# Phase one in chunks of 512 and 192 tokens, 112 rows of v, and a new order of the work

## The chip, the cores and the metric

The kernel runs on one core of a Trainium2 chip. Its time is device microseconds of one execution. TensorE (PE, its weight loads PEld), VectorE (DVE), ScalarE (ACT), GpSimd (POOL) and SyncE (SP) each work through a list of their own in order; DMA queues move the data.

## The reference, cut to what matters

```python
# attention: B, H, S, D = 4, 8, 576, 64; factor 4
out_d = sm_attn(mean4(q), mean4(k), mean4(v))      # 144 x 144 scores per head
out_local = sm_attn(q, k, v, |i - j| < 4)          # a band
x = repeat(out_d, 4) + out_local                   # then (B, S, 512)
# channel mix (phase one, and the gate of phase two)
xk = mu_k * x + (1 - mu_k) * x_prev
xr = mu_r * x + (1 - mu_r) * x_prev
v = relu(xk @ w_k) ** 2 @ w_v                      # 512 -> 1024 -> 512
x1 = sigmoid(xr @ w_r) * v
# conv GLU (phase two)
h = relu(x1 @ w_in)                                # 512 -> 1024
out = (h * sigmoid(conv3(h, conv_w))) @ w_out      # 1024 -> 512
```

All of it is float32 in and out, over 4 x 576 = 2304 tokens.

## The kernel before

**Stages.** The kernel first does the attention of batch 0 (heads in two groups, `gp`), in two pieces of 192 and 384 tokens. Phase one (`first_mix`, `mix`) multiplies by `w_k`, squares, multiplies by `w_v` and writes v to DRAM, in chunks of tokens: `chunks_` holds 192, 384 and then four of 432. The attention of batches 1 to 3 (`attend_batch`) runs between the matmuls of chunks 1 to 3. Phase two (`load_chunk`, `gate`, `hidden`, `outp`) reads x and v back and runs in five chunks of 384 or 512 tokens. In the first chunk the weights are used as float32 as they arrive (L919, L949). From the second on every product is made of three single-pass matmuls on a high and a low part of each operand (`for g, (wt, xs) in enumerate(((0, 0), (1, 0), (0, 1)))`), so a chunk of phase one has 96 matmuls in `up` (L983, 8 tiles of 12) and 96 in `down` (L1033, 4 tiles of 24, in halves), whatever its length; each has a weight load of 128x128 of its own. In phase two the lines are L1324 (gate), L1372 (hidden) and L1467 (out).

**Parts.** A weight block of 128x512 is read (L409), put together from two words by ScalarE and DVE (L396, L415, L399), copied to its high part on either engine (L435 or L437) and subtracted on DVE for the low part (L441). `mix_prep` forms xk of a chunk (L880 ScalarE, L888 DVE) and its two parts (L897, L902) in `late["xk"]`, one buffer. After `up` come relu (L1002), square, copy (L1014 or L1016) and subtraction (L1022) into the ring `k2` of nine buffers.

**Attention.** DVE sums keys and queries by four (L526). Scores (L564 band, L629 down-sampled) go through maxima, exponent and sums; transposes (L703, L759) land in PSUM and are copied by ScalarE (L709, L764). v comes as `vw`, 128 rows: two blocks of 64 positions, of which a block's window uses 38. For batch 0 a fold of `vw` by matmul (L499) replaces the sums by four; L786 and L805 are the products with v, L727 the down-sampled one, and its copy is L739.

**Order.** Each piece of work is a `step` with an engine, a cost and the keys that it reads and writes; the list `ORDER` gives the one order in which all steps are emitted, so that each engine's list follows from it. A step that may run on two engines runs on the second if its number stands in the set `SECOND`. DMAs are issued by the engine named in the step, nearly all by SP. Ten pieces of filler matmuls (L1089) stand in PE's list before the first scores.

**Memory.** `tmp` holds 8 tiles of NT tokens (a chunk's working tiles); `sq` the squares of chunk 0; `wr` the parts of `w_r`; at the end of the attention its pool is given up for phase two's weights, hidden tiles and a tile `v`.

Of the kernel before, what the change touches and what calls it, by code (L numbers as in the profile page):

```python
# [20 lines left out]
NFILL = 10  # L21


ORDER = [
# [178 lines left out]
def act(n):  # L203
    return 0.155 + 0.93e-3 * n
# [6 lines left out]
def pe(n):  # L211
    return 14.5e-3 + 0.4167e-3 * n
# [6 lines left out]
def tile_local_attention__then__channel_mix__then__conv_glu(  # L219
# [29 lines left out]
    NB = len(starts)  # L249
    PB = BQ // FAC  # L250
    NH = S // 3
    NT = 3 * S // 4
    ROW = -(-NT // 64) * 64
    chunks_ = [(0, NH), (NH, S - NH)] + [(t, NT) for t in range(S, B * S, NT)]
    K2 = 9
# [1314 lines left out]
```

## Time and profile before

| | us |
|---|---|
| median of three timed runs | 557.69 (556.16 to 558.6) |
| profiled execution, whole time | 556.9 |
| its span, first to last instruction | 554.8 |
| PE busy in the span | 538.7 |
| DVE busy | 366.3 |
| ACT busy | 300.3 |

The span is what the trace shows; 2.1 us of the profiled execution's time lie around it. Busy time is the time in which at least one instruction of the engine is under way. A matmul's record covers its whole passage through the array, so records overlap; the price of one in a dense stream is the distance between starts, which the chain of waits gives as a piece's length over its count.

### The profile page before, as it was taken

What the parts mean: (1) busy time and instruction counts of PE and PEld (TensorE: products, weight loads), DVE (VectorE), ACT (ScalarE), POOL (GpSimd) and SP (SyncE); (2) the same over time, 40 slices, a digit from 0 to 9 for tenths busy, and PEclk for the clock granted to TensorE, in tenths of its full rate; (3) what the DMA queues carried; (4) which work ended last, traced back from release to release, by engine and by line L of the source; (5) the groups of instructions that cost most, each with busy time, mean ns of one, the idle gap of its engine ahead of it and who ended that gap; (6) DMA issues with size and microseconds to landing.
All of it is one profiled execution on the core that took longest, in us unless ns stands there. A gap on an engine that the chain in (4) does not pass through costs nothing.

```text
span 554.8 us, 12885 instructions
## 1 busy us (share of the span) xinstructions
PE 538.7 (97%) x5364; PEld 479.4 (86%) x5364; DVE 366.3 (66%) x689; ACT 300.3 (54%) x676; POOL 43.5 (8%) x181
## 2 busy tenths in 40 slices
PE   6899899999999999999999999999999999999996
PEld 3788789899898999999999998888888888899985
DVE  4699897675675385456366698579747867766750
ACT  2888676356556555464566646455535443442441
POOL 5001010110101000000000001002001101100000
PEclk9999999999999999999999999999999999999999
DMA  8577883477364614413616022232022000010021
GB/s 325 209 249 205 331 252 104 125 236 223 91 207 126 193 60 142 143 57 129 223 38 222 34 76 77 76 115 95 1 64 107 19 1 2 0 58 21 0 77 57
DMA packets 25402, 66.14 MB, mean 119 GB/s; under 512 B 2688, under 2 KB 8320, under 8 KB 24320
## 3 DMA queue, kind: packets, MB, share of 16 engines
q1 hardware_dynamic: 23616, 62.37, 32.5%
q0 software_dynamic: 1728, 2.95, 3.2%
q8 instruction: 42, 0.69, 0.5%
q14 instruction: 16, 0.13, 0.1%
HBM read 51.15 MB, written 14.16 MB: 118 GB/s over the span
## 4 chain that ended last, share of the span: by engine, by line
PE 91%; DMA 3%; DVE 3%; ACT 1%; issue 1%; SPq 0%; ACTq 0%; DVEq 0%
PE a L1467 18%; PE mm L983 17%; PE mm L1033 17%; PE mm L1372 9%; PE a L1372 9%; PE mm L1324 4%; PE a L1324 4%; PE a L805 3%; PE mm L919 2%; DMA st_d<-in_moe_w_v 2%; DMA vw<-in_vw 2%; PE a L703 1%; PE a L727 1%; PE a L564 1%; PE a L759 1%; PE a L629 1%
## 5 line engine op out<-in xcount | busy, mean ns | idle before, releaser
L983 PE MATMUL mm<-xk,wk 128*128 128x432 f32 (+1 forms) x480 | 97.0, 357 | 0.8 <-issue 0.8
L1033 PE MATMUL mm<-k,wv 128*128 128x432 f32 (+1 forms) x480 | 95.6, 356 | 0.0
L1033 PEld LDWEIGHTS mm<-k,wv 128*128 128x128 f32 x480 | 88.3, 188 | 3.9 <-issue 0.7
L983 PEld LDWEIGHTS mm<-xk,wk 128*128 128x128 f32 x480 | 88.0, 188 | 4.1 <-issue 1.1
L1467 PE MATMUL a<-wk,wv 128*128 128x512 f32 x342 | 81.0, 389 | 0.0
L1467 PEld LDWEIGHTS a<-wk,wv 128*128 128x128 f32 x342 | 64.2, 188 | 13.3
L1372 PE MATMUL mm<-k,wi 128*128 128x512 f32 (+2 forms) x240 | 52.0, 368 | 0.0
L1372 PE MATMUL a<-k,wi 128*128 128x512 f32 (+2 forms) x240 | 51.9, 368 | 0.0
L1372 PEld LDWEIGHTS mm<-k,wi 128*128 128x128 f32 x240 | 44.0, 188 | 5.8
L1372 PEld LDWEIGHTS a<-k,wi 128*128 128x128 f32 x240 | 43.9, 188 | 5.6
L1439 ACT ACTIVATE tmp<-tmp 128x513 f32<-128x513 f32 (+1 forms) x40 | 23.6, 592 | 36.3 <-DVE tmp L1433 36.1
L1002 ACT ACTIVATE tmp<-mm 128x432 f32<-128x432 f32 (+1 forms) x40 | 20.8, 522 | 26.1 <-PE mm L983 11.8
L399 DVE SCALAR_TENSOR_TENSOR st_f<-st_f,st_d 128x512 uint32<-128x512 uint32 x28 | 19.3, 689 | 23.1 <-ACT st_d L415 23.1
L1442 DVE SCALAR_TENSOR_TENSOR tmp<-tmp,h 128x384 f32<-128x384 f32 (+3 forms) x64 | 26.9, 456 | 7.2 <-ACT tmp L1439 5.8
L1022 DVE TENSOR_TENSOR k<-tmp,k 128x432 fp32r<-128x432 f32 (+1 forms) x40 | 23.5, 595 | 9.9 <-ACT k L1014 8.8
L1433 DVE SCALAR_TENSOR_TENSOR tmp<-h,cw_sb,tmp 128x513 f32<-128x513 f32 (+1 forms) x40 | 28.0, 700 | 1.8
L1430 DVE SCALAR_TENSOR_TENSOR tmp<-h,cw_sb,tmp 128x513 f32<-128x513 f32 (+1 forms) x40 | 28.0, 700 | 1.8
L1453 DVE TENSOR_TENSOR wv<-tmp,wv 128x512 fp32r<-128x512 f32 (+1 forms) x32 | 20.0, 628 | 11.6 <-ACT wv L1451 11.4
L391 POOL DMA_DIRECT2D vd<-in_vp x18 | 14.7, 817 | 162.1 <-DMA vd<-in_vp 96.9
L1429 DVE TENSOR_SCALAR tmp<-h,cw_sb 128x513 f32<-128x513 f32 (+1 forms) x40 | 18.4, 460 | 12.2 <-ACT h L1409 11.3
L1482 ACT ACTIVATE st_d<-a 128x512 f32<-128x512 f32 x18 | 10.5, 595 | 27.4 <-PE a L1467 23.7
L1451 ACT CAST wv<-tmp 128x512 fp32r<-128x512 f32 (+1 forms) x32 | 17.9, 571 | 11.8 <-DVE tmp L1442 11.6
(174 smaller groups left out, 874.8 us busy)
## 6 DMA issues: line engine op xcount, KB each, us to landing
vw<-in_vw SPq DMA_DIRECT2D x7, 1152.0 KB, 6.5
kq<-in_kq SPq DMA_DIRECT2D x6, 1152.0 KB, 6.4
x_d<-xT SPq DMA_DIRECT2D x16, 288.0 KB, 3.4
out_dram<-st_d SPq DMA_DIRECT2D x18, 256.0 KB, 2.1
st_d<-in_moe_w_k SPq DMA_DIRECT2D x8, 512.0 KB, 4.3
st_d<-in_moe_w_v SPq DMA_DIRECT2D x8, 512.0 KB, 4.8
st_d<-in_moe_w_in SPq DMA_DIRECT2D x8, 512.0 KB, 3.8
st_d<-in_moe_w_out SPq DMA_DIRECT2D x8, 512.0 KB, 4.5
```

What stands on the lines that cost most here:

```text
L983: nc.tensor.matmul(pst[:, 0:n], lhsT=wk_t[wt][:, kt, mt * P:(mt + 1) * P], rhs=late["xk"][:, xs, kt, 0:n], start=(kt == 0 and g == 0), sto ...
L1002: lambda r=r, pst=pst: nc.scalar.activation(r, pst[:, 0:n], AF.Relu), (), [pk, rk],
L1022: lambda e, r=r, j=j: e.tensor_sub(late["k2"][1][:, j, 0:n], r, late["k2"][0][:, j, 0:n].bitcast(F32)),
L1033: nc.tensor.matmul(pst[:, 0:n], lhsT=wv_t[wt][:, kt, mt * P:(mt + 1) * P], rhs=late["k2"][xs][:, at[kt], 0:n], start=(kt == 0 and g == 0), ...
L1324: nc.tensor.matmul(pst[:, 0:n], lhsT=late["wr"][wt][:, kt, mt * P:(mt + 1) * P], rhs=r_t(c, xs, kt)[:, 0:n], start=(kt == 0 and g == 0), s ...
L1372: nc.tensor.matmul(pst[:, 0:n], lhsT=late["wi"][wt][:, kt, mt * P:(mt + 1) * P], rhs=x1s(xs, kt)[:, 0:n], start=(kt == 0 and g == 0), stop ...
L1430: nc.vector.scalar_tensor_tensor(out=cv, in0=tap(0), scalar=cw[:, 0, mt:mt + 1], in1=cv, op0=ALU.mult, op1=ALU.add)
L1433: nc.vector.scalar_tensor_tensor(out=cv, in0=tap(2), scalar=cw[:, 2, mt:mt + 1], in1=cv, op0=ALU.mult, op1=ALU.add)
L1439: step("ACT", act(m), lambda: nc.scalar.activation(cv, cv, AF.Tanh, scale=0.5), (), [cvk])
L1442: nc.vector.scalar_tensor_tensor(out=gf[:, o:q], in0=cv[:, o + j:q + j], scalar=1.0, in1=tap(1)[:, o + j:q + j], op0=ALU.add, op1=ALU.mult,)
L1453: ("DVE",), (dve(m),), lambda e: e.tensor_sub(gh_t(1, j)[:, 0:m], gf, gh_t(0, j)[:, 0:m].bitcast(F32)),
L1467: nc.tensor.matmul(pst, lhsT=xs[:, tt * P:(tt + 1) * P], rhs=wo[wt][:, kt, :], start=(kt == 0 and g == 0), stop=(kt == KF - 1 and g == 2),)
```

## The change

The chunks of phase one are 192, 384, 512, 512, 512 and 192 tokens (before: 192, 384 and four of 432). `k2` has eight buffers instead of nine, each now for 512 tokens. To make room, `w_r`'s parts move to a pool that opens when `sq` is given up, phase two's tile `v` and one of the two tanh buffers go to `tmp` and to the late pool. `vw` has 112 rows in DRAM and SBUF, and the fold uses those. `mus`, the mixing factors, are loaded over ScalarE's queue. For batch 0 the copies out of PSUM of the scores, the probabilities and the down-sampled output, and the scaling of chunk 0's x, may run on ScalarE or DVE. The planner's cost of a matmul is changed, and `ORDER` and `SECOND` are new lists.

In the first twelve DMAs of SP's list the order was: kq (both of group 0), kq (second half of group 0), kq (both of group 1), vw 0, vw 1, w_k 0, mus, kq (second half of group 1), w_k 2, w_k 1. It is now: kq (four pieces), vw 0, w_k 1, w_k 0, vw 1, w_k 2, and then the two second halves of kq; mus come over ScalarE. On DVE's list two sums of the second half's kq, the bits of w_k 3, the subtraction of w_k 2 and one block of maxima now stand before the last step of chunk 0's mix.

```diff
+VR = 112
 def pe(n):
-    return 14.5e-3 + 0.4167e-3 * n
+    return (13.4e-3 if n == 512 else 14.0e-3 if n in (382, 384) else 15.7e-3 if n > 300 else 11.6e-3) + 0.4167e-3 * n
...
-    NT = 3 * S // 4
+    NT = 4 * P
     ROW = -(-NT // 64) * 64
-    chunks_ = [(0, NH), (NH, S - NH)] + [(t, NT) for t in range(S, B * S, NT)]
-    K2 = 9
+    chunks_ = [(0, NH), (NH, S - NH)]
+    while chunks_[-1][0] + chunks_[-1][1] < B * S:
+        t = sum(chunks_[-1])
+        chunks_.append((t, min(NT, B * S - t)))
+    K2 = 8
...
+        def copy(eng, o, i):
+            if eng is nc.vector:
+                eng.tensor_copy(o, i)
+            else:
+                nc.scalar.copy(o, i)
+
+        def any_step(n, f, r, w, slack):
+            if b == 0:
+                step(("ACT", "DVE"), (act(n), 0.12 + 1.0e-3 * n), f, r, w, slack=slack)
+            else:
+                step("ACT", act(n), lambda: f(nc.scalar), r, w, slack=slack)
...
-            load(t.rearrange("p e h d -> p (e h d)"), vw[b, gp], NB // 2 * 4 * D, (), [k], SL[0])
+            load(t[0:VR].rearrange("p e h d -> p (e h d)"), vw[b, gp], NB // 2 * 4 * D * VR // P, (), [k], SL[0])
...
-                                pv[q:q + m, c], lhsT=z[:, 64 - o + q:64 - o + q + m],
-                                rhs=g["vw"][0][:, e].rearrange("p h d -> p (h d)"),
+                                pv[q:q + m, c], lhsT=z[0:VR, 64 - o + q:64 - o + q + m],
+                                rhs=g["vw"][0][0:VR, e].rearrange("p h d -> p (h d)"),
...
-                step("ACT", act((e - a) * P), cp, (), pks + [(ptk, a)], slack=SL[i0 > 0])
+                any_step((e - a) * P, cp, (), pks + [(ptk, a)], SL[i0 > 0])
...
-    step("SP", 0.2, lambda: nc.sync.dma_start(out=mus[:, 0:2], in_=mu), (), ["mus0"])
+    step("ACT", 0.45, lambda: nc.scalar.dma_start(out=mus[:, 0:2], in_=mu), (), ["mus0"])
...
-        late["wr"] = several(mid, 2, [P, KM, DM], F32R, "wr")
...
+    def open_wr():
+        sq_pool.release()
+        late["wrp"] = wrp = tc.alloc_tile_pool(name="wrp", bufs=1, reuse_waits="tile")
+        late["wr"] = several(wrp, 2, [P, KM, DM], F32R, "wr")
...
     def v_t(i, kt):
-        return cutout(st_d[1 + kt // 2], kt % 2 * CH, CH, F32) if i else late["v"][0][:, kt]
+        return cutout(st_d[1 + kt // 2], kt % 2 * CH, CH, F32) if i else tmp[:, kt]
...
+    def cv_t(i):
+        return cutout(tmp, KM * NT + 2 * CH, CH + 1, F32) if i else late["cv"][0]
```

## Rows read from the trace of the kernel before

**Rows 1.** The page's head: span, and busy time of the engines (share, instructions).

```profile
span 554.8 us, 12885 instructions
PE 538.7 (97%) x5364; PEld 479.4 (86%) x5364; DVE 366.3 (66%) x689; ACT 300.3 (54%) x676; POOL 43.5 (8%) x181
```

**Rows 2.** Stretches: from:to us, length, engines' busy us, granted clock, DMA share, GB/s.

```profile
4.00:12.00 8.00, 6.71 (x90) 3.40 (x93) 4.78 (x11) 1.20 (x5) 5.25 (x25) 1.00 1.00 382
12.00:24.00 12.00, 11.66 (x313) 9.07 (x315) 6.76 (x20) 7.91 (x23) 0.00 (x0) 1.00 0.65 252
...
28.25:55.00 26.75, 25.55 (x603) 23.06 (x601) 25.14 (x57) 22.66 (x60) 2.56 (x3) 0.96 0.73 226
55.00:77.00 22.00, 19.01 (x463) 17.02 (x458) 19.66 (x35) 16.28 (x41) 1.60 (x2) 1.00 0.83 294
...
27.00:30.40 3.40, 3.40 (x57) 2.96 (x50) 3.37 (x8) 1.49 (x5) 0.00 (x0) 0.53 0.83 272
```

**Rows 3.** Waits of PE: waiting line, what ended it, us in total, times, longest.

```profile
PE mm L499 <- DMA vw<-in_vw: 1.3, 1, 1.3
PE a L703 <- DVE pd L673: 1.3, 1, 1.3
```

**Rows 4.** The chain that ended last: start us, length us, what.

```profile
95.99 2.23 PE a L805 x144
...
210.12 18.80 PE mm L1033 x96
...
389.41 21.76 PE a L1467 x96
```

**Rows 5.** PE near 77 us (timeline), and L983's groups: busy, mean ns.

```profile
76.95 0.30 PEld L983 LDWEIGHTS mm<-xk,wk 128*128 128x128 f32 x2
76.95 0.44 PE L983 MATMUL mm<-xk,wk 128*128 128x384 f32 x1
...
L983 PEld LDWEIGHTS mm<-xk,wk 128*128 128x128 f32 x480 | 88.0, 188 | 4.1 <-issue 1.1
L983 PE MATMUL mm<-xk,wk 128*128 128x384 f32 x96 | 18.3, 340 | 0.8 <-issue 0.8
```

**Rows 6.** Groups of DVE and ACT by line and shape: busy us, mean ns.

```profile
L824 DVE COPY xT<-a 128x192 f32<-128x192 f32 x2 | 0.7, 359 | 1.3 <-PE a L805 1.3
L441 DVE TENSOR_TENSOR wk<-st_f,wk 128x512 fp32r<-128x512 f32 x12 | 8.3, 688 | 1.0 <-ACT wk L435 0.9
L437 DVE CAST wk<-st_f 128x512 fp32r<-128x512 f32 x5 | 2.1, 423 | 0.1
L526 DVE TENSOR_REDUCE kqd_f<-kq_f 128x96 f32<-128x384 f32 x2 | 1.1, 548 | 0.0
L888 DVE SCALAR_TENSOR_TENSOR tmp<-xT,mus,tmp 128x192 f32<-128x192 f32 x4 | 1.6, 413 | 0.0
L673 DVE TENSOR_TENSOR pd<-pd,sums 128x720 f32<-128x720 f32 x4 | 3.6, 904 | 0.1
L709 ACT COPY pdt<-a 80x768 f32<-80x768 f32 x2 | 1.6, 788 | 1.3 <-PE a L703 1.3
L709 ACT COPY pdt<-a 80x512 f32<-80x512 f32 x2 | 1.2, 581 | 1.7 <-PE a L703 1.7
L764 ACT COPY pt<-a 128x512 f32<-128x512 f32 x14 | 8.3, 590 | 5.2 <-PE a L759 5.2
L764 ACT COPY pt<-a 128x256 f32<-128x256 f32 x2 | 0.8, 375 | 0.0
```

**Rows 7.** DMA issues up to 18 us: KB each, median us to landing.

```profile
vw<-in_vw SPq DMA_DIRECT2D x1, 1152.0 KB, 8.7
mus<-in_mu SPq DMA_DIRECT2D x1, 4.0 KB, 11.3
```

**Rows 8.** PE's timeline around the first matmul on weights: start us, us.

```profile
23.70 0.90 PE L805 MATMUL a<-pt,vw_f 38*64 38x32 f32 x48
...
28.25 0.69 PE L919 MATMUL mm<-tmp,st_f 128*128 128x192 f32 x1
```

More of the change, by code (lines that the diff above doesn't have):

```diff
@@ L380, in tile_local_attention__then__channel_mix__then__conv_glu, with load @@
     step("POOL", 4.7, make_picks, (), ["picks"])
-    def load(o, i, words, r, w, slack=1.0, rows=P):
-        step("SP", dma_us(words, rows), lambda: nc.sync.dma_start(out=o, in_=i), r, w, slack=slack)
+    def load(o, i, words, r, w, slack=1.0, rows=P, k=1.0):
+        step("SP", k * dma_us(words, rows), lambda: nc.sync.dma_start(out=o, in_=i), r, w, slack=slack)
     def load_sum(o, planes, words, keys, slack, rows=P):
@@ L471, in loads @@
                     len(prs) * (e - a), (),
-                    [(k, i, pr) for pr in prs for i in ({0, half} if whole else {i0})], SL[i0 > 0],
+                    [(k, i, pr) for pr in prs for i in ({0, half} if whole else {i0})], SL[i0 > 0], P, 1.0,
                 )
@@ L706, in down_out, with cp @@
                 step("PE", 0.218 * (e - a) + TAIL, f, [(pdk, 0), (pdk, 1)], pks, slack=SL[i0 > 0])
-                def cp(a=a, e=e, pv=pv):
-                    nc.scalar.copy(
-                        pdt[:, :, a:e].rearrange("p k c s -> p k (c s)"), pv[:HC, :, 0:(e - a) * P]
-                    )
-                step("ACT", act(2 * (e - a) * P), cp, (), pks + [(pdtk, a)], slack=SL[i0 > 0])
+                def cp(eng, a=a, e=e, pv=pv):
+                    copy(eng, pdt[:, :, a:e].rearrange("p k c s -> p k (c s)"), pv[:HC, :, 0:(e - a) * P])
+                any_step(2 * (e - a) * P, cp, (), pks + [(pdtk, a)], SL[i0 > 0])
             if b == 0 and i0 == 0:
@@ L736, in down_out, with cp @@
             whole = m // BQ * BQ
-            def cp():
-                nc.scalar.copy(od[:, :, 0:whole], po[:, :, 0:whole])
+            def cp(eng):
+                copy(eng, od[:, :, 0:whole], po[:, :, 0:whole])
                 if m > whole:
-                    nc.scalar.copy(od[:, :, whole:m], po[:, :, nq * BQ - (m - whole):nq * BQ])
-            step("ACT", act(2 * whole), cp, (), pks + [odk], slack=SL[i0 > 0])
+                    copy(eng, od[:, :, whole:m], po[:, :, nq * BQ - (m - whole):nq * BQ])
+            any_step(2 * whole, cp, (), pks + [odk], SL[i0 > 0])
         def local_out(i0, i1):
@@ L761, in local_out, with cp @@
                 step("PE", 0.109 * (e - a) + TAIL, f, g["sk", i0], pks, slack=SL[i0 > 0])
-                def cp(a=a, e=e, pst=pst):
-                    nc.scalar.copy(pt[:, a:e].rearrange("p i r -> p (i r)"), pst[:, 0:(e - a) * P])
-                step("ACT", act((e - a) * P), cp, (), pks + [(ptk, a)], slack=SL[i0 > 0])
+                def cp(eng, a=a, e=e, pst=pst):
+                    copy(eng, pt[:, a:e].rearrange("p i r -> p (i r)"), pst[:, 0:(e - a) * P])
+                any_step((e - a) * P, cp, (), pks + [(ptk, a)], SL[i0 > 0])
             over = b == 0 and i0 == 0
@@ L875, in mix_prep, with scaled @@
             xs = [("xT", b % 2, kt, c) for b, a, e in parts for c in (0, half) if (c == 0 or e > NH)]
-            def scaled(t=t, kt=kt):
+            def scaled(eng, t=t, kt=kt):
                 for b, a, e in parts:
                     o = b * S + a - t0
-                    nc.scalar.activation(
-                        t[:, o:o + e - a], xT[b % 2][:, kt, a:e], AF.Copy, scale=mus[:, 2, kt:kt + 1])
-            step("ACT", act(n) + 0.1 + 0.3 * (len(parts) - 1), scaled, xs + ["mus"], [tk])
+                    to, by, m = t[:, o:o + e - a], xT[b % 2][:, kt, a:e], mus[:, 2, kt:kt + 1]
+                    if eng is nc.vector:
+                        eng.tensor_scalar_mul(to, by, m)
+                    else:
+                        nc.scalar.activation(to, by, AF.Copy, scale=m)
+            if i == 0:
+                step(("ACT", "DVE"), (act(n) + 0.1, dve(n)), scaled, xs + ["mus"], [tk])
+            else:
+                step(
+                    "ACT", act(n) + 0.1 + 0.3 * (len(parts) - 1),
+                    lambda scaled=scaled: scaled(nc.scalar), xs + ["mus"], [tk],
+                )
             def whole(t=t, f=f, kt=kt):
@@ L1115, in tile_local_attention__then__channel_mix__then__conv_glu @@
     late["two"] = True
-    by_columns(w_r, lambda: late["wr"][0], lambda: late["wr"][1], KM, range(KM), "wr", ["mid"])
+    def open_wr():
+        sq_pool.release()
+        late["wrp"] = wrp = tc.alloc_tile_pool(name="wrp", bufs=1, reuse_waits="tile")
+        late["wr"] = several(wrp, 2, [P, KM, DM], F32R, "wr")
+    step("", 0.0, open_wr, ["mid"], [k for k in prog.writer if root(k) == "sq"] + ["wrp"])
+    by_columns(w_r, lambda: late["wr"][0], lambda: late["wr"][1], KM, range(KM), "wr", ["wrp"])
     store_x(0)
@@ L1139, in tile_local_attention__then__channel_mix__then__conv_glu @@
     att_keys = [k for k in prog.writer if root(k) in names]
-    sq_keys = [k for k in prog.writer if root(k) == "sq"]
     def open_late():
-        sq_pool.release()
         att.release()
-        late["low"] = low = tc.alloc_tile_pool(name="low", bufs=1, reuse_waits="tile")
-        late["v"] = several(low, 1, [P, KM, CH], F32, "v")
         wb = late["pool"] = tc.alloc_tile_pool(name="wb", bufs=1, side="right", reuse_waits="tile")
@@ L1151, in open_late @@
         late["edge"] = several(wb, 1, [P, KF, ahead + 1], F32, "edge")
-        wb.tile([P, 72], F32, name="gap2")
-    step("", 0.0, open_late, (), att_keys + sq_keys + ["late"])
+        late["cv"] = several(wb, 1, [P, CH + 1], F32, "cv")
+        wb.tile([P, 192], F32, name="gap2")
+    step("", 0.0, open_late, ["wrp"], att_keys + ["late"])
     class Late:
@@ L1204, in r_t @@
     def r_t(c, x, kt):
-        if c == 0:
-            return late["xk"][:, x, kt]
-        if 4 * x + kt < 6:
-            return cutout(late["xk"], (KM * x + kt) * CH, CH, F32R)
-        return cutout(late["k2"][0], (KM + kt - 2) * CH, CH, F32R)
+        return late["xk"][:, x, kt]
     def x1s(x, kt):
-        return cutout(late["k2"][x], 64 * x + kt * CH, CH, F32R)
+        return cutout(late["k2"][x], kt * CH, CH, F32R)
     def v_t(i, kt):
-        return cutout(st_d[1 + kt // 2], kt % 2 * CH, CH, F32) if i else late["v"][0][:, kt]
+        return cutout(st_d[1 + kt // 2], kt % 2 * CH, CH, F32) if i else tmp[:, kt]
     def v_dst(i):
@@ L1219, in v_dst @@
             return [(2 * j, 2 * j + 2, flat(st_d[1 + j], F32).rearrange("p (k c) -> p k c", k=2)) for j in range(2)]
-        return [(0, KM, late["v"][0])]
-    v_old = ("late", "st_old")
+        return [(0, KM, tmp[:, 0:KM])]
+    v_old = ("tmp_lo", "st_old")
     xrf = [cutout(xT[1], CH * i, CH, F32) for i in range(2)]
@@ L1225, in tile_local_attention__then__channel_mix__then__conv_glu @@
     os_t = [cutout(st_d[0], DM * i, DM, F32) for i in range(2)]
-    cv_t = [cutout(tmp, (CH + 1) * i, CH + 1, F32) for i in range(2)]
-    gt_t = [cutout(tmp, 2 * (CH + 1) + CH * i, CH, F32) for i in range(2)]
+    gt_t = [cutout(tmp, KM * NT + CH * i, CH, F32) for i in range(2)]
+    def cv_t(i):
+        return cutout(tmp, KM * NT + 2 * CH, CH + 1, F32) if i else late["cv"][0]
     GB = 10
@@ L1233, in gh_t @@
         i = 2 * (j - KF) + x
-        return cutout(late["k2"][1], 64 + (KM + i - 1) * CH, CH, F32R) if i else cutout(late["k2"][0], (KM + 2) * CH, CH, F32R)
+        return cutout(late["k2"][1], (KM + i - 1) * CH, CH, F32R) if i else cutout(late["k2"][0], (KM + 2) * CH, CH, F32R)
     step("", 0.0, lambda: None, (), [k for k in prog.writer if k[0] == "xT" and k[1] == 0] + ["xc"])
@@ L1239, in tile_local_attention__then__channel_mix__then__conv_glu @@
     step("", 0.0, lambda: None, (), keys_of("k2") + ["k2_old"])
+    step("", 0.0, lambda: None, (), [k for k in prog.writer if k[0] == "tmp" and k[1] < KM] + ["tmp_lo"])
     step("", 0.0, lambda: None, (), keys_of("tmp") + ["tmp_old"])
@@ L1302, in load_chunk @@
             step("DVE", 0.13 + 1.27e-3 * n, whole, [("xc", "d"), ("xc", "pad")], [fk])
-            old = ["xk_old"] + (["k2_old"] if c else [])
+            old = ["xk_old"]
             step(
@@ L1423, in hidden @@
         parts = [0] + [t - outs[c][0] for t in seam] + [m]
-        cv, cvk = ring("cv", cv_t)
+        ci, cvk = ring("cv", (0, 1))
         gt, gk = ring("gt", gt_t)
-        cv, gf = cv[:, 0:m + gap], gt[:, 0:m]
+        gf = gt[:, 0:m]
         def conv():
+            cv = cv_t(ci)[:, 0:m + gap]
             nc.vector.tensor_scalar_mul(cv, tap(1), cw[:, 1, mt:mt + 1])
@@ L1437, in hidden, with tanh @@
         hks = [(hk, "pad"), (hk, "d")]
-        step("DVE", 0.43 + 3.36e-3 * m, conv, hks + ["cw", "tmp_old"], [cvk])
-        step("ACT", act(m), lambda: nc.scalar.activation(cv, cv, AF.Tanh, scale=0.5), (), [cvk])
+        step("DVE", 0.43 + 3.36e-3 * m, conv, hks + ["cw", "tmp_old", "late"], [cvk])
+        def tanh():
+            cv = cv_t(ci)[:, 0:m + gap]
+            nc.scalar.activation(cv, cv, AF.Tanh, scale=0.5)
+        step("ACT", act(m), tanh, (), [cvk])
         def glu():
+            cv = cv_t(ci)
             for j, (o, q) in enumerate(zip(parts, parts[1:])):
@@ L1508, in tile_local_attention__then__channel_mix__then__conv_glu @@
     late["pool"].release()
-    late["low"].release()
+    late["wrp"].release()
     late["mid"].release()
@@ L1539 @@
         .reshape(B, H // 4, 4, len(starts) // 2, 2, 64, D)
-        .transpose(0, 1, 4, 5, 3, 2, 6).reshape(B, H // 4, P, -1)
+        .transpose(0, 1, 4, 5, 3, 2, 6).reshape(B, H // 4, P, -1)[:, :, 0:VR]
     )
```

167 rows, old and new, of tables (ORDER, SECOND) are left out of this document.

## Prediction

> **What bounds the kernel now.** I read the page's head first: PE is busy for 97% of the span [rows 1], so a gain has to be either fewer nanoseconds per matmul or less waiting before PE's stream closes. Then the table of stretches [rows 2]: from 4 to 77 us PE has holes (8.00 us hold 6.71 us of work, 26.75 hold 25.55, 22.00 hold 19.01), while DVE is full from 28 to 77 us (25.14 of 26.75 and 19.66 of 22.00, 92%); before 24 us DVE is idle for 3.2 and 5.2 us. The front is thus bound by DVE, with PE close behind. The list of PE's waits names single waits of about a microsecond, no repeated one [rows 3]. From about 100 us the chain of waits is PE alone: whole passes of 96 matmuls at 432 tokens take 18.80 us (195.8 ns each; five such pieces stand in a row), and at 512 columns 21.76 us (226.7 ns) [rows 4]. Columns alone would be 180.0 and 213.3 ns at 2.4 GHz, so the price over them is 15.8 and 13.3 ns. The tail behind the last matmul is not touched. The profiled execution took 556.9 us, 2.1 more than its span; the median of the three timed runs is 557.69, 0.8 above it. The sum is made against 556.9, and 0.5% (2.8 us) is about what a measurement can tell from no change.
>
> **Part 1, the chunks.** Each chunk of phase one is 192 matmuls, whatever its length. Removed: four chunks of 432, 8 x 18.80 = 150.4 us. Added: three of 512, 3 x 192 x 226.7 ns = 130.6 us, and one of 192. What a single-pass matmul of 192 columns costs stands in no row; the fewest single-pass columns so far are 382.
>
> What matters is the weight load in front of every matmul. Where PE had been waiting, two loads of 128x128 stand alone: together they take 0.30 us, one takes 188 ns, so the second began 0.11 us after the first; the matmul between them took 0.44 us instead of its usual 340 ns, 0.10 longer, because it stood waiting for its weights [rows 5]. Feeding 128 columns of weights thus takes about 110 ns. Behind 384 or more columns (160 ns) that is hidden; behind 192 columns (80 ns) it isn't, if, as here, a load begins when the matmul before it begins. Then the pitch is the load's: 111 ns, and the chunk takes 192 x 111 = 21.3 us. Lower bound: the columns plus the 14 ns seen at 512 and 432, 94 ns, 18.0 us. Upper bound: the transposed-probability products load 64 columns for few moving ones; 144 take 2.23 us, 15.5 ns each, four tiles side by side, so 62 ns per load of 64 columns [rows 4] and 124 ns for 128, 23.8 us. I take 111, the row with the same tile shape.
>
> [...]
>
> Sum of part 1: 130.6 + 21.3 - 150.4 = **+1.5 us** (between -1.8 and +4.0). All of it lies on the path, since nothing but PE stands in the chain there.
>
> Behind the short chunk, less time covers what follows. The last hidden tile goes through relu, square, copy and subtraction, about 0.36 us each at 192 columns (as the DVE copy of 128x192), with another subtraction of up to 0.69 us in DVE's queue [rows 6]: about 2.1 us. The two first half-sums of the second product cover it with 2 x 12 x 0.111 = 2.7 us. I take 0, at most 1. Phase two's preparation has 96 x 0.111 = 10.7 us of cover instead of 18.8, for some 4.1 us of DVE steps (two mix steps and four subtractions, 0.69 each at most): 0. One k2 buffer fewer: its next write comes a whole tile (12 x 0.227 = 2.7 us) after the matmuls that free it: 0. The v tile in tmp, the new pool for w_r and the tanh buffer are used long after their space is free: 0; without that cover it would be one landing, at most the 8.7 us of the largest transfer [rows 7].
>
> **Part 2, the first loads.** SP issues the first v (vw) after four kq pieces instead of five, and v has 112 rows instead of 128: 384 KB and 144 KB less ahead of its landing, at the 382 GB/s of that stretch [rows 2] 1.4 us sooner than the 8.7 us now [rows 7]. PE waits for it once, 1.3 us [rows 3]. But the transposes that come before the fold in the new order hang on DVE's softmax steps, and DVE now takes a kq sum of the second head group (768 columns; one of 384 takes 0.55 us [rows 6]) ahead of the first group's maxima. So what is late next is DVE, not the v load. The mixing factors (mus, 4 KB) need 11.3 us to land on SP's queue [rows 7]; on ScalarE's queue they pass nothing, ScalarE has no work there, and their reader on DVE stands behind some 15 us of DVE's list: 0 either way. Moved behind the weights, the second halves of kq have no reader before about 20 us: 0. Fewer rows don't shorten PE's fold, whose matmuls keep their columns.
>
> **Part 3, copies and order, the front.** I compared the two lists engine by engine. DVE takes over in the front: the fold's copy (2 x 0.38), two score copies (0.58, 0.79), three probability copies (0.59, 2 x 0.38), one of down-sampled output (0.36), one of x (0.36), one scaling (0.41), two weight copies (2 x 0.42) and a square (0.36), 5.8 us [rows 6]. It gives ScalarE three weight copies and one normalisation, 3 x 0.42 + 0.90 = 2.2 us. Net 3.6 us more on the engine that is full. Against that the new order pulls work ahead of the first matmul on weights (L919): two kq sums (2 x 0.55), a weight's bits, a weight's subtraction and a block of maxima (about 0.69 each): 3.2 us, done where DVE now idles. Of the copies taken over, 2.5 us lie in that idle stretch too, and 3.3 behind it. Behind the first weight matmul DVE therefore has 3.2 less, 3.3 more and 2.2 less to do: 2.1 us less.
>
> When does that matmul start? Now at 28.25, behind the last first-half output that begins at 23.70 [rows 8]. In the new order I put that output's end at 23.6 instead of 24.6 (the earlier v); behind it DVE has a copy (0.36), five mix steps (5 x 0.41) and three of 0.69: 4.5 us, so 28.1. The same, give or take half a microsecond. So the front gains at most 2.1 x 0.92 = 1.9 us; I take **-1.5 us**, leaving 0.4 for a ScalarE order that puts weight conversions ahead of probability copies. Bounds: -5 (the 4.2 us of PE's holes between 28 and 77 us gone too, and some of the half clock) to +3.6 (nothing pulled forward helps). The clock stands at 0.53 from 27.0 to 30.4 us [rows 2], the 1.2 GHz level for nearly all of it, behind holes on PE; that costs up to 1.6 us. The new list keeps a hole there, of some 2.5 us before L919, so I charge no change.
>
> Sum: 556.9 + 1.5 - 1.5 = **556.9 us**.
>
> **The rivals.** *A, the load hides:* the weights come in time and the last chunk costs columns plus 14 ns: 18.0 us, part 1 is -1.8, total 553.6. For it: PE loads ahead of running matmuls everywhere. Against it: the 0.11 us spacing was seen with nothing else in the array. [...] *B, the front closes:* DVE's lead lets PE's 4.2 us of holes and part of the half clock go, front -5: 553.4. For it: those waits are short and hang on DVE and ScalarE. Against it: PE and DVE are both nearly full, and weights still arrive over a queue that is busy. *C, DVE becomes tighter:* the 3.6 us of copies move to the full engine between 12 and 77 us, and what was pulled forward merely waits for data; front +3.6, total 562.0. It decides at 28 us: if L919 starts later than about 29, C holds. Against it: DVE's 8 us of idle before 24.
>
> **How the numbers follow.** Forecast (load-bound last chunk, small front gain) 0.47, own range 554 to 559.5; A 0.20; B 0.18; C 0.15. The range runs from 552.5, below A and B, to 560.5, leaving most of C and A's far end outside. Faster by over 0.5%: two thirds of A and B, a little of the forecast, 0.29. Slower: most of C and a few of the forecast, 0.16. Same: 0.55.
>
> **What would show it.** The last chunk: 96 matmuls of 192 columns near 10.7 us (A: 9.0) at 2.4 GHz; a chunk of 512 at 43.5. The front: first L919 near 28 us, first L983 near 75.5 instead of 76.95 (B: 72, C: 80). PE without a hole from the last chunk into L1324. The prediction is wrong if the last chunk leaves PE waiting for ScalarE or DVE, or if a new wait opens while batches two and three's attention run beside the longer chunks.

## The result, and the profile after

The changed kernel takes 564.24 us (median of four runs, 562.56 to 565.19); the kernel before, run beside it, 558.02. The ratio is 1.0114, 95% interval 1.0079 to 1.0149: 6.2 us slower, where 556.9 was forecast and 560.5 was the end of the range. Runs of one kernel lie 2 to 6 us apart, so what follows rests on ratios (3 to 12 runs of a kernel), and single traces say where, not how much. One run of a_432 (1357 us) and one of b_shift (582.6) count as slow and stand in no ratio. The profiled execution after took 562.56 us.

Its head, then the stretches of [rows 2] (same columns; ... marks lines left out):

```profile
span 560.8 us, 12892 instructions
PE 541.7 (97%) x5364; PEld 465.2 (83%) x5364; DVE 372.1 (66%) x700; ACT 296.1 (53%) x661; POOL 45.4 (8%) x181
```

```profile
4.00:12.00 8.00, 7.46 (x158) 4.54 (x158) 6.83 (x17) 1.54 (x8) 5.16 (x25) 1.00 1.00 283
12.00:24.00 12.00, 8.93 (x157) 5.82 (x158) 6.97 (x20) 6.18 (x15) 0.00 (x0) 0.90 1.03 335
...
28.25:55.00 26.75, 23.83 (x548) 21.16 (x542) 25.16 (x59) 21.17 (x54) 2.56 (x3) 1.00 0.64 198
55.00:77.00 22.00, 20.33 (x423) 18.18 (x423) 18.83 (x35) 17.41 (x45) 0.80 (x1) 0.92 0.86 271
```

In 4 to 12 us the DMA engines are as busy as before (share 1.00) and move 283 GB/s instead of 382. In 12 to 24 us PE works 8.93 us where it worked 11.66. PE's waits (total, times, longest) and the first loads (KB, us from issue to landing), which answer to [rows 3, 7]:

```profile
PE mm L1057 <- ACT pd L673: 1.8, 1, 1.8
PE mm L516 <- DMA vw_f<-in_vw: 1.5, 1, 1.5
...
PE a L581 <- issue: 1.0, 1, 1.0
```

```profile
vw<-in_vw SPq DMA_DIRECT2D x1, 1008.0 KB, 10.0
vw_f<-in_vw SPq DMA_DIRECT2D x1, 1008.0 KB, 16.5
mus<-in_mu ACTq DMA_DIRECT2D x1, 4.0 KB, 9.3
```

The first v, an eighth smaller and issued earlier, lands later: 10.0 us after its issue instead of 8.7. The second (vw_f) lands 16.5 us after its issue, at 20.8. The chain that ended last (start, length) holds that load, then the chunks:

```profile
4.28 16.48 DMA vw_f<-in_vw
...
244.37 21.76 PE mm L1007 x96
266.12 21.76 PE mm L1057 x96
287.89 10.70 PE mm L1007 x96
298.58 10.72 PE mm L1057 x96
```

A chunk of 512 costs 43.5 us, the last one 21.4, 111.5 ns per matmul, and in the chain phase two follows at 309.30, where the last piece ends, without a hole. So the chunks' matmuls went as computed, and the larger part of the loss has to lie elsewhere: the first matmul on weights starts at 31.7 us (28.3 before), phase two, whose first record overlaps the last piece, at 309.1 (304.0).

### The profile page after: what moved, and what is told of

The parts are those of the page before. It is cut to its first block, busy times and chain, and to the rows that moved or that the text cites. A ratio compares the mean times of both kernels' runs of the same rounds, so it can differ in the third digit from the quotient of the medians.

```text
span 560.8 us, 12892 instructions
## 1 busy us (share of the span) xinstructions
PE 541.7 (97%) x5364; PEld 465.2 (83%) x5364; DVE 372.1 (66%) x700; ACT 296.1 (53%) x661; POOL 45.4 (8%) x181
## 4 chain that ended last, share of the span: by engine, by line
PE 86%; DMA 8%; DVE 3%; issue 1%; ACT 1%; SPq 1%; ACTq 0%; POOLq 0%
PE mm L1057 17%; PE a L1501 17%; PE mm L1007 15%; PE mm L1398 9%; PE a L1398 9%; PE mm L1350 4%; PE a L1350 4%; DMA vd<-in_vp 4%; DMA vw_f<-in_vw 3%; PE a L820 2%; PE a L581 1%; PE a L742 1%; PE a L720 1%; PE a L646 1%; PE mm L973 1%
## 5 line engine op out<-in xcount | busy, mean ns | idle before, releaser
L1057 PE MATMUL mm<-k,wv 128*128 128x512 f32 (+2 forms) x480 | 97.5, 359 | 1.8 <-ACT pd L673 1.8
L1007 PE MATMUL mm<-xk,wk 128*128 128x512 f32 (+2 forms) x480 | 96.6, 358 | 0.0
L1057 PEld LDWEIGHTS mm<-k,wv 128*128 128x128 f32 x480 | 80.7, 189 | 13.5 <-issue 2.4
L1007 PEld LDWEIGHTS mm<-xk,wk 128*128 128x128 f32 x480 | 80.9, 189 | 11.9 <-issue 0.5
L1026 ACT ACTIVATE tmp<-mm 128x512 f32<-128x512 f32 (+2 forms) x40 | 20.8, 523 | 39.0 <-PE mm L1007 24.6
L1046 DVE TENSOR_TENSOR k<-tmp,k 128x512 fp32r<-128x512 f32 (+2 forms) x40 | 23.5, 595 | 12.3 <-ACT k L1038 11.4
L1350 PE MATMUL mm<-xk,wr 128*128 128x512 f32 (+2 forms) x120 | 25.9, 369 | 0.0
L1350 PE MATMUL a<-xk,wr 128*128 128x512 f32 (+2 forms) x120 | 25.7, 369 | 0.0
L401 ACT ACTIVATE st_f<-st_d 128x512 f32<-128x512 f32 x28 | 18.8, 671 | 10.5 <-DVE wi L446 5.4
L1350 PEld LDWEIGHTS a<-xk,wr 128*128 128x128 f32 x120 | 22.0, 188 | 2.8
L1350 PEld LDWEIGHTS mm<-xk,wr 128*128 128x128 f32 x120 | 21.9, 188 | 2.8
L420 ACT ACTIVATE st_d<-st_d 128x512 uint32<-128x512 uint32 x36 | 23.8, 660 | 0.0
```

Source lines behind the costliest of these rows:

```text
L401: nc.scalar.activation(f, high.bitcast(F32), AF.Prelu, scale=2.0 ** -112, alpha=2.0 ** 32)
L420: nc.scalar.activation(low, low, AF.Copy, bias=-0.5, scale=2.0 ** -29 * (1.0 - 2.0 ** -20))
L1007: nc.tensor.matmul(pst[:, 0:n], lhsT=wk_t[wt][:, kt, mt * P:(mt + 1) * P], rhs=late["xk"][:, xs, kt, 0:n], start=(kt == 0 and g == 0), sto ...
L1026: lambda r=r, pst=pst: nc.scalar.activation(r, pst[:, 0:n], AF.Relu), (), [pk, rk],
L1046: lambda e, r=r, j=j: e.tensor_sub(late["k2"][1][:, j, 0:n], r, late["k2"][0][:, j, 0:n].bitcast(F32)),
L1057: nc.tensor.matmul(pst[:, 0:n], lhsT=wv_t[wt][:, kt, mt * P:(mt + 1) * P], rhs=late["k2"][xs][:, at[kt], 0:n], start=(kt == 0 and g == 0), ...
```

## The experiments

Ratios are to the kernel before on the same chip. The three other columns are starts in the one profiled execution: first matmul on weights (L919 before, L943 after), first up-matmul of chunk 1 (L983, L1007), phase two. A front that is the same in two kernels starts its matmuls on weights at 27.8 in one trace and 29.5 in the other (a_v128_432, a_v128), with 112 rows at 34.3 and 31.7 (a_432, after): a start in one trace is worth that much.

| kernel | ratio (95% interval) | weights | chunk 1 | phase two |
|---|---|---|---|---|
| before | 1 | 28.3 | 77.0 | 304.0 |
| after | 1.0114 (1.0079 to 1.0149) | 31.7 | 79.7 | 309.1 |
| before, v in 112 rows (b_v112) | 1.0104 (1.0071 to 1.0137) | 32.3 | 82.5 | 310.9 |
| after, v in 128 rows (a_v128) | 1.0018 (0.9993 to 1.0044) | 29.5 | 78.6 | 307.2 |
| after, 128 rows for batch 0 only (a_late112) | 1.0040 (1.0021 to 1.0059) | 28.8 | 76.3 | 305.3 |
| after, old order and engines in the front (a_front) | 1.0160 (1.0125 to 1.0195) | 31.5 | 81.6 | 312.3 |
| after, chunks of 432 (a_432) | 1.0102 (1.0069 to 1.0134) | 34.3 | 83.7 | 310.1 |
| after, 128 rows, chunks of 432 (a_v128_432) | 1.0001 (0.9975 to 1.0027) | 27.8 | 73.8 | 300.8 |
| a_v128, 120 more instructions (a_v128_shift) | 1.0310 (1.0276 to 1.0344) | 32.4 | 87.1 | 322.6 |
| before, 120 more instructions (b_shift) | 1.0325 (1.0296 to 1.0353) | 30.1 | 90.0 | 322.3 |
| a_v128, one half-sum moved (a_v128_swap) | 1.0034 (1.0007 to 1.0061) | 28.6 | 76.5 | 305.7 |
| a_v128_432, one score step moved (a_best) | 0.9963 (0.9944 to 0.9983) | 29.2 | 76.1 | 301.7 |

**The 112 rows, taken out of the change and put alone into the kernel before.** The theory: the load itself is slow. The rival: order and copies delay the front.

```diff
-VR = 112
+VR = 128
```

> The changed kernel with v loaded in 128 rows again, nothing else touched. Theory T (the load of 112 rows is slow: 547 ns for a packet of 9216 bytes against 351 ns at 128 rows, and the front waits for it): the first v lands 1 to 2 us sooner, the second (vw_f) at about 15 to 17 us instead of 20.8, the first matmul on weights (L943) starts at 28.5 to 29.5 us instead of 31.7, and the time falls by 2 to 3 us, to 561.2 to 562.2. Rival O (the new order and the copies on DVE delay the front): the load lands sooner but L943 stays within 0.7 us of 31.7, and the time stays within 1 us of 564.2.

```diff
-load(t.rearrange("p e h d -> p (e h d)"), vw[b, gp], NB // 2 * 4 * D, (), [k], SL[0])
+load(t[0:112].rearrange("p e h d -> p (e h d)"), vw[b, gp], NB // 2 * 4 * D, (), [k], SL[0])
...
-    .transpose(0, 1, 4, 5, 3, 2, 6).reshape(B, H // 4, P, -1)
+    .transpose(0, 1, 4, 5, 3, 2, 6).reshape(B, H // 4, P, -1)[:, :, 0:112]
```

> The kernel before with v loaded in 112 rows, the one part alone; order, engines and chunks as before. Theory T (slow load): packets of 9216 bytes take about 550 ns, the first v lands 1.5 to 3 us later, the first matmul on weights (L919) moves from 28.25 to 30 to 31.5 us, and the time rises by 2 to 3 us, to 560 to 561. Rival O (order and copies): the time stays within 1 us of 558.0, and L919 within 0.7 us of 28.25.

Both point the same way, and further than expected. Without the 112 rows the change costs 0.18% instead of 1.14%, 5.3 us less (3 to 8 by the two intervals); alone in the kernel before, they cost 1.04%, 5.8 us. In the trace of a_v128 the two v land 8.6 and 14.0 us after their issue, not 10.0 and 16.5. And the starts fall into two groups: in the four kernels with 112 rows throughout the matmuls on weights begin at 31.5 us or later, in the six with 128 rows for batch 0 and an unshifted stream at 29.5 or earlier. The stretches and waits of b_v112 show how:

```profile
4.00:12.00 8.00, 6.29 (x87) 3.27 (x87) 4.75 (x11) 1.14 (x5) 5.25 (x25) 1.00 1.03 296
12.00:24.00 12.00, 10.09 (x194) 6.50 (x195) 5.50 (x17) 4.58 (x15) 0.00 (x0) 0.72 0.80 250
```

```profile
PE mm L499 <- DMA vw<-in_vw: 3.6, 1, 3.6
PE a L703 <- DVE pd L673: 3.0, 1, 3.0
PE mm L983 <- issue: 2.3, 1, 2.3
```

PE waits 3.6 us for the first v (1.3 before) and then runs in part at a lower clock: the granted clock is 0.72 instead of 1.00 over 12 to 24 us, and a matmul of the fold takes 634 ns instead of 379. The matmuls on weights begin 4.0 us late, and by phase two it is 7.0. Of this, 1.8 us come from the wait ahead of L983 that the list gives to "issue": it ends at 88 us and is 2.7 us from start to start, where the kernel before has one of 0.8. What such gaps are comes below.

```diff
+n = 112 if b else 128
-load(t[0:VR].rearrange("p e h d -> p (e h d)"), vw[b, gp], NB // 2 * 4 * D * VR // P, (), [k], SL[0])
+load(t[0:n].rearrange("p e h d -> p (e h d)"), vw[b, gp, 0:n], NB // 2 * 4 * D * n // P, (), [k], SL[0])
```

> The changed kernel with v in 128 rows for batch 0 (the two loads that the front waits for) and in 112 rows for batches 1 to 3. If the price of the 112 rows is paid in the front alone, the time is that with 128 rows throughout, ratio 1.000 to 1.003 to the kernel before. If the six later loads pay too (they share queue and engines with the weights and the next batch's scores), it lies between: 1.004 to 1.009.

1.0040: most of the price (1.0114 to 1.0040, 4.1 us) is paid by batch 0's two loads. The six later ones cost 0.2%, which these intervals cannot tell from nothing; 1.0040 is the lower edge of what was expected if they pay too.

**The order, put back in the front.** All steps up to chunk 1 in the old order on the old engines; 112 rows and the rest as changed.

> The changed kernel with the order and the engines of the kernel before for all steps up to the first matmul of chunk 1; 112 rows, chunks and the later order as changed. Rival O (order and copies delay the front): the first matmul on weights comes back to 28 to 29.3 us and the time falls by 2.5 to 3.5 us, to 561. Theory T (slow v load): the front stays late, at 30.5 to 32 us, and the time stays within 1 us of 564.2.

The front stays late (31.5 us) and the time is higher still, 1.0160. The copies on DVE and the order are not what delayed it. That the ratio is above 1.0114 is not clear of the noise, and a gap of 2.0 us of the kind described below, at 87 us, is part of it.

**The load by itself.** One load at a time, then four in flight.

```diff
+ts = [get(f"{name}{i}") for i in "abcd"]
+for i, t in enumerate(ts):
+    nc.sync.dma_start(out=t[0:n, :], in_=src[n * i:n * i + n])
```

> Only loads, one at a time and then four in flight, all the rest of the computation is left out (the output is zeros): rows of 9216 bytes, 128, 120, 112, 96, 80 and 64 of them into the first partitions, 112 as a load of 64 and one of 48, 112 from rows that lie 9728 bytes apart in memory, 112 into partitions 16 to 127, and 128 rows of 8064 bytes (as many bytes as 112 of 9216). Theory T1 (a load is dealt out to 16 engines in equal runs of rows, and runs of 7 rows go badly together where runs of 8 and of 4 do not): 112 alone takes longer than 128 alone although it carries an eighth less, by up to the 1.37 times seen in the first loads (7.66 against 5.61 us of the 16 engines' time); 96 and 80 rows are slow per byte too, 64 rows is fast; 64 plus 48 lies between; 112 from rows farther apart stays slow. Theory T2 (where the rows lie in memory): 112 is slow only at the pitch of 9216 and fast at 9728. Theory T3 (the loads are slow in the kernel only because of what else is in flight there): 112 alone takes 0.875 of the time of 128, and four of them too.

> Only loads again, the computation left out (the output is zeros): four loads in flight each time, rows of 9216 bytes, 128, 120, 112 and 96 rows, then 64, 64 plus 48, 32 and 80. Theory T1 (the load is dealt out to the engines in equal runs of rows, and only runs that fill the ports evenly reach full speed): 128 reaches 420 GB/s, 64 and 32 nearly as much per byte once they are queued; 112, 96 and 80 stay near 290 GB/s; 64 plus 48 lies between 290 and 420. Rival T4 (the number of rows as such: fewer rows, fewer ports): the rate falls evenly with the rows, 96 at three quarters and 64 at half of that of 128.

DVE's timeline of the first (a copy behind each landing; four of 128 rows, then four of 112), and of the second (120 rows, then 64):

```profile
192.99 0.15 DVE L75 COPY zero<-f128b 128x1 f32<-128x1 f32 x1 [2.63 <-DMA f128b<-in_vw]
195.78 0.15 DVE L75 COPY zero<-f128c 128x1 f32<-128x1 f32 x1 [2.63 <-DMA f128c<-in_vw]
...
209.10 0.15 DVE L75 COPY zero<-f112b 128x1 f32<-128x1 f32 x1 [3.61 <-DMA f112b<-in_vw]
212.80 0.15 DVE L75 COPY zero<-f112c 128x1 f32<-128x1 f32 x1 [3.54 <-DMA f112c<-in_vw]
```

```profile
28.41 0.15 DVE L68 COPY zero<-xb 128x1 f32<-128x1 f32 x1 [5.02 <-DMA xb<-in_vw]
33.56 0.15 DVE L68 COPY zero<-xc 128x1 f32<-128x1 f32 x1 [5.00 <-DMA xc<-in_vw]
...
222.24 0.15 DVE L68 COPY zero<-wb 128x1 f32<-128x1 f32 x1 [2.68 <-DMA wb<-in_vw]
225.07 0.15 DVE L68 COPY zero<-wc 128x1 f32<-128x1 f32 x1 [2.68 <-DMA wc<-in_vw]
```

From the first landing to the second and from the second to the third, rows of 9216 bytes, and the rate that this makes (all such spacings of both runs; the fourth of four comes sooner behind the third, with 128 rows hardly):

| rows | 128 | 120 | 112 | 96 | 80 | 64 | 32 | 64 + 48 |
|---|---|---|---|---|---|---|---|---|
| us | 2.75 to 2.93, mostly 2.79 | 5.15 to 5.26 | 3.38 to 3.77, once 4.58 | 3.44 to 3.62 | 3.09 to 3.28 | 2.83 to 3.06 | 1.44 to 1.46 | 5.34 to 5.53 |
| GB/s | 403 to 429, mostly 423 | 210 to 215 | 274 to 305, once 225 | 244 to 257 | 225 to 239 | 193 to 208 | 202 to 205 | 187 to 193 |

One load at a time (DVE's wait for it, three of each): 128 rows 5.1 to 5.4 us, 112 rows 5.6 to 5.9, 112 at a pitch of 9728 bytes 5.9 to 6.3, 112 into partitions 16 to 127 6.0 to 6.2, and 128 rows of 8064 bytes, as many bytes as 112 of 9216, 4.8 to 5.4. So 112 rows take longer than 128 with no other work in the program, which strikes out T3, at either pitch, which strikes out T2, and it is the rows, not the bytes. T1 has 112, 96 and 80 rows slow, and they are, but 96 and 80 lie at 225 to 257 GB/s and not near its 290, and it fails for 64 and 32, which it had near full speed: they run at half of it. Nor is the rate even in the rows, as T4 had it: 120 rows are slower than 112, and 32 run at the rate of 64. Of the sizes tried only 128 rows came over 400 GB/s. Why the others land where they do (which engine writes which rows isn't in the trace, and the ports of T1 and T4 show in no run) stays open.

**The chunks.**

```diff
-chunks_.append((t, min(NT, B * S - t)))
+chunks_.append((t, min(432, B * S - t)))
```

> The changed kernel with four chunks of 432 tokens in place of 3 of 512 and one of 192; order, copies, loads as changed. If the last chunk's pitch of 111 ns is the whole price of the chunks, phase one gets 1.5 us shorter: 562.7. The wait of 1.8 us near 212 us, ahead of the second product of chunk 3, is the other thing beside the chunks: if it hangs on the longer chunk (more of ScalarE's work queued ahead), it goes too and the time is 560.9; if it is a matter of the order or of the instruction stream it stays, at 562.7.

> The changed kernel with v in 128 rows and four chunks of 432 tokens: of the change there remain the order, the copies on either engine and the factors over ScalarE's queue. Against the kernel before, the front is 0.5 to 1.5 us late (first matmul on weights 28.8 to 29.8 us) and the wait of 1.8 us ahead of chunk 3's second product is still there; the part from the first matmul of the second product of chunk 1 to phase two takes 203.4 us as in the other kernel with 432, against 205.8 with 512: total 0.5 below to 1 us above the kernel before. If the chunks were free (no load-bound pitch) it would be as the kernel with 128 rows alone, 1 to 2 us above.

With 432 instead of 512 and 192 the ratio falls by 0.0012 and by 0.0017, 0.7 and 0.9 us, each with an uncertainty of some 2. The traces are sharper: from chunk 1's first down-matmul (L1057) to phase two it is 203.4 and 204.1 us with chunks of 432, 205.8 with 512 in both partners. The wait of 1.8 us stays, ahead of the same matmul, with either chunk (1.7 and 2.0 us with 432); so it doesn't hang on them. And the order, the copies, the buffers and the factors over ScalarE's queue together come to 1.0001: nothing that an interval of 1.5 us to either side can show.

**The wait that the chunks don't explain.** Here is the end of the changed kernel's scores near 211 us, and a line of the old-order kernel at the same place:

```profile
210.94 0.84 PE L581 MATMUL a<-kq 64*32 64x38 f32 x59
213.57 0.40 PE L1057 MATMUL mm<-k,wv 128*128 128x512 f32 x1 [1.80 <-ACT pd L673]
```

```profile
216.43 0.23 PE L590 MATMUL a<-kq 64*32 64x38 f32 x2 [1.70 <-issue]
```

The list of waits names a softmax step on ScalarE. But that step stands behind this product in `ORDER`, and the product doesn't need it. By the keys of the steps the last thing that the product needs of ScalarE is a relu (L1026), and the last of these ahead of the gap began at 210.30 us and took 0.60. In the second kernel the gap sits two matmuls ahead, before a score matmul that waits for nothing ("issue"). What both have in common is a count: 7,105 of PE's records (weight loads, matmuls and the few semaphore and drain instructions of its own, by start) lie ahead of the first one behind the gap, and 7,105 is 27 x 256 + 193. Counted in the same way:

| kernel | gaps (us, start to start, and where they end) at 193 + n x 256 |
|---|---|
| after | 1.2 at 58, 1.9 at 214 |
| a_front | 2.0 at 87, 1.9 at 216 |
| b_v112 | 2.7 at 88 |
| a_v128_shift | 2.0, 1.2, 1.0, 5.2, 1.3, 1.7, 5.3: 17.6 in all |
| b_shift | 0.9, 1.7, 4.9, 3.5, 2.1, 1.3: 14.4 in all |

Every gap that the list gives to "issue" there with 1 us or more is of this kind; waits for data have other remainders. And the DMA records hold a queue named instruction whose packets are 16,384 bytes long; the changed kernel has 42 of them, one for every 256 of PE's 10,756 records. The rows for 210.6 to 211.0 us (packets, MB, share):

```profile
q8 instruction: 1, 0.02, 18.8%
```

In all 18 gaps of the table PE resumes 2.3 to 3.0 us after the start of such a packet. The run of short instructions ahead of the gap is 376 long (188 matmuls with their loads). The changed kernel has two more of that length, at 107 and 159 us, and the kernel before one at 103; none of those three shows a gap. Only in the one at 209 us do two borders lie, so that a whole block of 256 is used up in 1.7 us. One kind of test moves the borders of the blocks and little else (60 matmuls and loads come on top), by cutting the filling matmuls at the start into narrower ones; another leaves the borders and breaks up the run.

```diff
-for _ in range(2):
-    nc.tensor.matmul(mm_t[1][:, 0:8 * W], lhsT=ident16, ...)
+for i in range(8):
+    nc.tensor.matmul(mm_t[1][:, 2 * W * (i % 4):2 * W * (i % 4) + 2 * W], lhsT=ident16, ...)
```

> The changed kernel with v in 128 rows, and each of the ten filling steps at the start in 8 matmuls of 76 columns instead of 2 of 304: the same columns, 60 more matmuls with 60 more weight loads, so everything behind stands some 120 instructions later in PE's stream; order and data as they were. Theory F (the stall of 1.8 us ahead of chunk 3's second product is PE's instruction supply, used up by some 350 short instructions in 2.5 us): the stall leaves that instruction, for another place in the same run of short ones or for none, and the time is 0 to 1.8 us less than with 128 rows alone. Rival W (it waits for ScalarE, as the list of waits names it): it stays ahead of the first matmul of that product, 1.7 to 1.8 us long, and the time is as with 128 rows alone.

> The kernel before with its ten filling steps in 8 matmuls of 76 columns each instead of 2 of 304: the same columns, 120 more instructions in PE's stream ahead of everything, nothing else. Theory F: the borders of the 256-instruction blocks move to other matmuls; from the trace of before, with a block needing 3.55 us behind the last border, the stalls sum to 8.2 us (1.9 near 55 us, 1.5 near 76, 2.4 near 105, 1.6 near 122, 0.3 to 0.4 at two others), and the time rises by 6 to 12 us. Rival (what the changed kernel lost with the same shift was its order, not the shift): the time rises by at most 1 us, the price of 60 short matmuls at the start.

The gap at 211 us is gone in the first, but there are seven others of about 1 us and more, and the time rose by 2.9%, where at most no change was expected: the mechanism held, the sign of the sum did not. In the kernel before, where the borders' movement had been worked through, 6 to 12 us were expected and 18 came. Its waits:

```profile
PE a L564 <- issue: 10.5, 4, 4.7
...
PE a L629 <- issue: 3.0, 3, 1.4
```

The gaps make 14.4 us instead of the 8.2 worked out, through ones like that of 4.9 us that ends at 66.2: its packet began only at 63.8, 2.5 us after PE had run dry at 61.3. Why it began so late is not shown. Beside the gaps the granted clock is lower, 0.90 instead of 0.98 from 28 to 77 us and 0.94 instead of 1.00 from 77 to 130.

```diff
-... 685 (scores), 691 (scores), 686 (scores), 630 (half-sum) ...
+... 685 (scores), 630 (half-sum), 691 (scores), 686 (scores) ...
```

> The changed kernel with v in 128 rows and one step moved: the first half-sum of chunk 3's second product (12 matmuls, 2.7 us) stands ahead of the last 64 of batch 3's score matmuls instead of behind them, so the run of short matmuls is cut in two. Theory F (instruction supply): the stall of 1.76 us is gone or under 0.5 us, the time 1.3 to 1.8 us less than with 128 rows alone. Rival W (a wait for ScalarE's softmax): the step now stands before that softmax's last scores and either waits as long, 1.7 us, or the stall moves to the next half-sum.

The half-sum went ahead of 104 score matmuls (40 down-sampled and 64 of the band), not of the last 64 alone. No gap at a border is left there, but the transposes behind now wait for data (1.71 us for L1035, which is this kernel's L1026), and nothing is won: 1.0034.

```diff
-... 621 (a tile of the first product), 685 (scores), 691, 686, 630 ...
+... 685 (scores), 621 (a tile of the first product), 691, 686, 630 ...
```

> The changed kernel with v in 128 rows, four chunks of 432, and one step moved: the 79 score matmuls of batch 3's second head group stand ahead of the last first-product tile of chunk 3 instead of behind it, so that no run of more than 300 short instructions is left there. Theory F (PE's instruction supply comes in blocks of 256 and a block used up in less than about 3.5 us leaves PE waiting): the stall of 2.0 us ahead of chunk 3's second product is under 0.4 us, and the time 1.5 to 2 us less than with 128 rows and 432 alone: ratio 0.9965 to the kernel before. Rival W (a wait for ScalarE's softmax): the stall stays, there or at the transposes behind it, 1.5 us or more, ratio 1.0000.

```profile
197.94 0.82 PE L590 MATMUL a<-kq 64*32 64x38 f32 x60
198.69 2.62 PE L1066 MATMUL mm<-k,wv 128*128 128x432 f32 x12
```

The half-sum follows the scores without a gap, and the ratio is 0.9963 (0.9944 to 0.9983): 2.1 us faster than the kernel before. From chunk 1's first down-matmul to phase two it takes 202.6 us where the same kernel without the move takes 204.1. It is the change with v in 128 rows, chunks of 432 and this one step moved, and it beats both kernels, the one before by 0.4%.

## Why the prediction was wrong, point by point

**Part 2 is the step that failed.** It took 384 and 144 KB off the load's way at 382 GB/s, the rate of that stretch [rows 2], and got 1.4 us sooner. That rate belonged to loads of 128 rows. A load of 112 carries an eighth less at 0.7 of the rate, and it landed at 12.7 us instead of 11.8. Part 2 also looked at the first v only; the second, which lands at 20.8 us, is the one in the chain. "So what is late next is DVE, not the v load" put the part at 0 in the sum; it cost 5.3 us taken out, 5.8 put in alone. The loads alone show the two rates, 423 GB/s with 128 rows and about 290 with 112. The fold cost the same with either: 380 ns a matmul with the first v in 112 rows as in 128.

**Part 1 held.** 111.5 ns where 111 was taken, no hole into phase two, +1.6 us by the matmuls; taken out (a_432, a_v128_432) the traces give 2.4 and 1.7 and the times 0.7 and 0.9, all within its bounds. Rival A is out. No row gives the 2.4 GHz of the columns; by both traces matmuls start 174 ns apart (median) at 384 columns and 227 at 512, so a column more costs 0.41 ns, 2.4 columns a ns.

**In part 3 a term was missing.** -1.5 us was forecast, 0.1 measured (a_v128_432), with 1.5 to either side. With the gap near 198 us taken away it is -2.1 (a_best): what the forecast summed up may thus be right, and a gap of 2 us that it had no term for took it back. Runs of 376 short instructions were in both lists; no row had priced one, and that a whole block falls into the new one is a matter of position. The order was read for what it waits for, not for how fast it is eaten. A sign of it stood in the waits of the kernel before, in a line that [rows 3] doesn't show:

```profile
PE mm L983 <- issue: 0.8, 2, 0.5
```

These two are gaps at borders, which end at 81 and 100 us. The line also belies "single waits" and "no repeated one".

The half clock, for which no change was charged, moved: between 10 us and phase two it is one stretch granted 0.50 in the kernel before, from 26.8 to 30.2 us, in which L919's matmuls start 320 ns apart (163 at 1.00), and two in the changed kernel, from 21.6 to 24.9 and from 72.8 to 76.1 us.

**Rival C met its mark for another reason.** "If L919 starts later than about 29, C holds": it started at 31.7, and the time came out 2.2 us above C's 562.0. But DVE was not the cause (a_front). A milestone that two causes can delay does not tell them apart; the landing of v would have.

**The wait forecast as a danger came.** "If a new wait opens while batches two and three's attention run beside the longer chunks": it is the one of 1.8 us at 211; the longer chunks had nothing to do with it.

In sum, along the chain of kernels from before over a_v128_432 and a_v128 to after: order and copies 0.1 us (their gap of 2.0 included), chunks 0.9, 112 rows 5.3, each with an uncertainty of 1.5 us or more.

## What to carry to other kernels

Bytes saved are time saved only at an unchanged rate: a transfer whose shape changes is priced by a row of the new shape, and here fewer rows took longer (112 rows 3.38 to 3.77 us, 128 mostly 2.79). When a wait names a step that had long ended, or "issue", count the engine's instructions up to it: a run of short matmuls, 188 here, outran its own instruction stream where a whole block fell into it (1.9 us at 214), and 12 matmuls of 432 columns in its midst left no gap (a_best). A shift of the stream (120 instructions here), run beside a reordered kernel, tells luck of position from merit of order.

## What the runs showed of the hardware that was not expected

**Rows per load.** Of the sizes tried only 128 rows got 423 GB/s; 120 got 215, less than 112 with about 290, and half the rows got half the rate (64: 208); a quarter of them got no less (32: 205).

**Instruction supply.** 42 packets of 16 KB came in the changed kernel, as many blocks of 256 as PE's 10,756 records fill (10,728 matmuls and weight loads, 28 semaphore and drain instructions), and PE stands still at a block's border when the block before it was used up too fast: 1 to 5.3 us a time, 14 to 18 us in a kernel shifted by 120 instructions. How fast is too fast is not one figure: in the twelve kernels' traces each of the 12 blocks used up in 1.7 us or less had a gap of 1.7 to 5.3 us behind it, blocks used up in 1.8 and 2.0 us had none (a_v128_shift), and one used up in 4.7 us had 2.7 (b_v112). The kernel before stood well by luck of position: its largest such gap was 0.8 us, at 81. Behind matmuls that start 14 ns apart (59 in 0.84 us above) the border cost 1.9 us.
